# Weight splitting without a scaling pass and without a GpSimd subtraction, and a new table of ranks for the order of the work

## The chip, the cores and the metric

The kernel runs on one core of one Trainium2 chip. The core has five engines that run side by side, each through its own list of instructions in a fixed order: TensorE (PE, matrix products), VectorE (DVE) and ScalarE (ACT) for element-wise work, GpSimd (POOL), and SyncE (SP), which here only starts transfers (DMAs). Semaphores make an instruction wait for another engine's result. The metric is the time on the device of one execution, in microseconds (us); shown are the median of three timed executions and one more execution that was profiled.

## The reference

Two stages run one after the other. The first filters each of 8 sequences in the frequency domain; the second sends each of the 19968 rows through one of 8 small networks.

```python
# first stage: x is (8, 2496, 256)
X = np.fft.rfft(x, axis=1)
Yr = Xr @ w_r - Xi @ w_i + b_r
Yi = Xr @ w_i + Xi @ w_r + b_i
Yr, Yi = (sign(Y) * maximum(abs(Y) - 0.01, 0) for Y in (Yr, Yi))
y = np.fft.irfft(Yr + 1j * Yi, n=2496, axis=1)
# second stage: x = y as (19968, 256); w1 is (8, 256, 1024), w2 is (8, 1024, 256)
logits = x @ w_gate
e = argmax(logits, axis=1);  gate = softmax(logits)[row, e]
out[row] = gate * (maximum(x[row] @ w1[e], 0) @ w2[e])
```

## The kernel before, in words

Each sequence is a batch b of 0 to 7. Its transform of length 2496 is factored as 39 x 64, so that it is two matrix products in a row with a store to HBM and a load in another layout between them. Products that need more than half precision are made from a high and a low float16 part of each operand, three products instead of one.

The steps of a batch, with the lines of the functions and the engine: `s1` (L480, PE) is the first transform in six pieces, `s1_out` (L487, ACT) takes it from PSUM, `s1_store` and `zload` (L493, L498, SP) carry it through HBM. Then five pieces per batch run through a chain: `s2` (L509, PE); `s2_hi` (L514, ACT), `s2_lo` (L519, DVE) and `s2_neg` (L525, ACT), which split its result; `wmul` (L537 to L539, PE, 48 products), the weights of the filter; `thr` (L546, DVE), `thr_pos` (L552, ACT), `thr_sub` (L558, DVE), `thr_out` (L564, ACT) and `thr_lo` (L569, POOL), the threshold and the split for the way back; `inv1` (L585 to L587, PE), `inv1_hi` (L592, ACT), `inv1_lo` (L597, DVE), and `vstore` (L602, SP). When the five pieces of a batch are stored, `inv2` (L638, PE) makes the second inverse transform, `ytrans` and `logits` the gate's products, `route1` to `route3` find each row's expert and place, and 22 `scatter` instructions (L758, POOL) write the rows to HBM in the order of experts. `table` (DVE) then says which rows a block of 256 takes.

The second stage has 71 blocks of 256 rows and 21 of 128. A block is `fetch_x` (L944) and `fetch_w` (L935, the expert's weights, only where the expert changes), `up` (L980 to L982, 24 or 48 products), `up_relu` (ACT), `up_hi` and `up_lo` (DVE), `down` (L1008 to L1010, 24 products), `down_gate` (ACT) and `down_store` (L1019, POOL). Blocks 0 to 11 need batches 0 and 1, blocks 12 to 21 batch 2 as well, and so on; the first block can start when two batches are routed and all weights are split.

The weights of the 8 experts are split beside the first stage, in 16 units u of 1 MB: `wprep_load` (L778, SP), `wprep_sq` (L783, ACT, a sum of squares), `wprep_sum` (L787, PE), `wprep_scale` (DVE, a power of two), and for each half of the unit `wprep_mul` (L804, DVE: times the power of two, in place), `wprep_hi` (L808, ACT: the float16 part), `wprep_lo` (L812, POOL: the rest) and `wprep_store` (L817, SP).

The order on every engine is made before the program is built, by a planner (`Plan.run`): it keeps a list of ready tasks for each engine and starts the one of lowest rank when the engine is free, with a duration and buffers given for each task. A DMA of a rank above 0 waits while the modelled transfer queue is longer than `BACK`. The order that comes out is what the engines run; on the chip an engine that waits holds everything behind it. The load of weight unit u is not ready before `WT0 + WTD * u`, and the loads of the second inverse for batches from 2 on not before `INV0 + INVD * (b - 2)`.

Of the kernel before, what the change touches and what calls it, by code (L numbers as in the profile page):

```python
# [13 lines left out]
AF = mybir.ActivationFunctionType  # L14
ALU = mybir.AluOpType
# [17 lines left out]
def blocks(B):  # L33

    NT = B * NSEQ
    NF = -(-(NT - NE * 255) // 256)
    NB = NF + (NT + NE * 127) // 128 - 2 * NF
    tabs, j0 = [], 0  # L40
    for m, n in sorted(EPOCHS.items()):
        if m < B:
            tabs.append((m, j0, n - j0, 256))
            j0 = n
    tabs += [(B, j0, NF - j0, 256), (B, NF, NB - NF, 128)]
    slot, pos = [], []
    for t, (_, j0, n, _) in enumerate(tabs):
        k = KS if j0 >= JS else 2
        sl = [j % k for j in range(j0, j0 + n)]
        p, at = [0] * n, 0  # L50
        for s in range(k):
            own = [i for i in range(n) if sl[i] == s]
            for q, i in enumerate(own if t % 2 == 0 else own[::-1]):
                p[i] = at + q
            at += len(own)
        slot += sl
        pos += p
    return NF, NB, tabs, slot, pos
# [73 lines left out]
EPOCHS = {2:12,3:22,4:31,5:41,6:51,7:61}  # L132
JS, NPRE = 12, 2
SCD = 2.6
INV0, INVD, WT0, WTD = 430, 90, 60, 24
EV = -1
FILL = 430
ZD = 3
# [12 lines left out]
class Plan:  # L151


    LAT, DLAT, BACK = 0.2, 2.0, 4.0

    def __init__(self, bufs):
        self.t, self.bufs, self.mark = [], bufs, {}
# [2 lines left out]
        return Buf(name)  # L160

    def add(self, eng, dur, f, *a, deps=(), rank=0, take=(), free=(), dma=0.0, name=None, after=0.0, prev=None, lag=0.0):
        t = dict(eng=eng, dur=dur, f=f, a=a, deps=[d for d in deps if d is not None], rank=rank, take=take, free=free,
                 dma=dma, i=len(self.t), after=after, name=name, prev=prev, lag=lag)
        for b in free:
            b.left += 1
        self.t.append(t)
        if name is not None:
            self.mark[name] = t
        return t  # L170
# [86 lines left out]
def build(ctx: ExitStack, tc: tile.TileContext, x, w_r, w_i, b_r, b_i, wg, w1, w2,  # L257
# [3 lines left out]
    V, S, P, T, Q = nc.vector, nc.scalar, nc.gpsimd, nc.tensor, nc.sync  # L261
# [9 lines left out]
    NF, NB, TABS, SLOT, _ = blocks(B)  # L271
# [164 lines left out]
    st = {}  # L436
# [361 lines left out]
    def wparts_of(u, i):  # L798
        return (st[("ws", u)][:, 1024 * i:1024 * i + 1024],
                wt[u % 2][1][:, i, :].rearrange("p (l c) -> p l c", l=2))  # L800

    def wprep_mul(u, i):
        wi, _ = wparts_of(u, i)
        V.tensor_scalar(wi, wi, st[("wn", u)][:, 1:2], None, op0=ALU.mult)  # L804

    def wprep_hi(u, i):
        wi, wo = wparts_of(u, i)
        S.activation(wo[:, 0, :], wi, AF.Copy)  # L808

    def wprep_lo(u, i):  # L810
        wi, wo = wparts_of(u, i)
        P.tensor_tensor(wo[:, 1, :], wi, wo[:, 0, :], ALU.subtract)  # L812

    def wprep_store(u, i):
        e, w = divmod(u, 2)
# [213 lines left out]
    A = L.add  # L1029
# [44 lines left out]
    def ns_(c):  # L1074
        return min(4, SLOTS - 4 * c)
# [2 lines left out]
    wst_ = {}  # L1078
    for u in range(2 * NE):
        wa, wb = L.buf(f"wt{u % 2}0"), L.buf(f"wt{u % 2}1")  # L1080
        ld = A("SP", 1.0, wprep_load, u, take=[wa], dma=3.4, rank=0.5, after=WT0 + WTD * u)
        sq = A("ACT", 2.5, wprep_sq, u, deps=[ld], rank=0)
        sm_ = A("PE", 0.2, wprep_sum, u, deps=[sq, wst_.get(("sc", u - 1))], rank=-100)
        scl = wst_["sc", u] = A("DVE", 1.5, wprep_scale, u, deps=[sm_], rank=0, take=[wb])
        for i in range(2):
            m_ = A("DVE", 1.1, wprep_mul, u, i, deps=[scl], rank=0)
            h = A("ACT", 1.05, wprep_hi, u, i, deps=[m_], rank=0)
            l = A("POOL", 2.3, wprep_lo, u, i, deps=[h], rank=0, free=[wa])
            wst_[u, i] = A("SP", 0.5, wprep_store, u, i, deps=[l], dma=1.7, rank=0, free=[wb])
    wdone = [t for k, t in wst_.items() if k[0] != "sc"]  # L1090

# [1 line left out]
    for b in range(B):  # L1093
        F = 10 * b

        ld = [] if b else ld0
        for c in range(6):
            if b:
                ld.append(A("SP", 1.3, load_x, b, 4 * c, 4 * c + ns_(c), deps=[s1l[b - 1, c], nps[b - 1][c]],
                            rank=0.3, dma=8.0 * ns_(c) / 22))  # L1100
# [9 lines left out]
        for c in range(6):  # L1110
# [3 lines left out]
                              rank=F - 9.5, take=[pb_, zb] + ([zdb] if not c else []))  # L1114
            l = A("ACT", 1.05 * k, s1_out, b, c, deps=[t], free=[pb_], rank=EV)
# [3 lines left out]
        for i in range(5):  # L1119
# [3 lines left out]
            h = A("ACT", 1.11, s2_hi, b, i, deps=[t, xs], rank=EV)  # L1123
            l = A("DVE", 1.28, s2_lo, b, i, deps=[h], free=[p2_], rank=EV)
# [9 lines left out]
            h = A("ACT", 1.01, inv1_hi, b, i, deps=[v1], rank=EV)  # L1134
            l = A("DVE", 1.22, inv1_lo, b, i, deps=[h], free=[pa_], rank=EV)
# [10 lines left out]
        for c in range(6):  # L1146
# [5 lines left out]
                  take=[pb_, yr_], free=[vs_], rank=I + 2, lag=0.0 if pre else 6.0)  # L1152
            h = A("ACT", 1.12 * k, inv2_hi, b, c, deps=[t, ys], rank=EV)
            l = A("DVE", 1.28 * k, inv2_lo, b, c, deps=[h], free=[pb_], rank=EV)
# [39 lines left out]
    for j in range(NB):  # L1194
# [3 lines left out]
                       take=[xb_[j], tb_[j]], dma=1.95 if j < NF else 0.98, rank=0 if j < js else 1.2 + j * 1e-3, prev=ft.get(j - 1))  # L1198
        for w in range(2):
            wb_[j, w] = L.buf(f"wt{SLOT[j]}{w}")  # L1200
            wl[j, w] = A("SP", 0.8, fetch_w, j, w, deps=[tabs[ep]] + (wdone if j < 2 else []) + ([sw] if j >= js else []),
                         take=[wb_[j, w]], dma=1.3, rank=0 if j < js else 1.1 + j * 1e-3 + w * 5e-4,
                         prev=wl.get((j - 1, w)))
    for k, (kind, j, q) in enumerate(seq):
        if kind == "u":
# [3 lines left out]
            if q == 0:  # L1209
# [4 lines left out]
                             free=[xb_[j], wb_[j, 0]], rank=M + k)  # L1214
# [3 lines left out]
        else:  # L1218
# [3 lines left out]
                  free=hs_ + [wb_[j, 1]], rank=M + k)  # L1222
# [23 lines left out]
```

## Time and profile before

| | |
|---|---|
| timed executions | 1453.88, 1455.05, 1458.22 us; median 1455.05 us |
| profiled execution | 1445.12 us, span on the core 1442.9 us |
| PE busy | 1383.2 us, 96% of the span |
| DVE busy | 872.7 us, 60% |
| ACT busy | 696.8 us, 48% |
| POOL busy | 540.2 us, 37% |

The span is what lies between the first and the last instruction on the core; 2.2 us of the profiled execution lie around it. The profiled execution is 9.9 us under the median of the timed ones. The first block's `up` starts at 516.74 us; before that point the core works mainly on the first stage and the weights, after it mainly on blocks.

### The profile page before, as it was taken

Reading aid. Unit: us, or ns where it says so; the run is one execution under the profiler, and the core shown is the slowest. Engines: PE = TensorE matmul, PEld = TensorE weight load, DVE = VectorE, ACT = ScalarE, POOL = GpSimd, SP = SyncE. Lnnn points to the kernel's source line nnn. Section 1 sums busy time; section 2 is a strip of 40 time slices with the busy share of each in tenths; the row PEclk is TensorE's granted clock in tenths of the full one; section 3 lists DMA queues with packets and bytes.
Section 4 is the critical chain, followed back from the end, with each engine's and each line's share of the span. In section 5 each row is a group of like instructions: output and inputs, shape, how many; then the busy total and the mean of one; then the engine's idle time right before and its main releaser. Section 6 shows DMA issues by size and latency. Waiting matters only on the chain.

```text
span 1442.9 us, 33059 instructions
## 1 busy us (share of the span) xinstructions
PE 1383.2 (96%) x12682; PEld 1176.1 (82%) x12682; DVE 872.7 (60%) x1744; ACT 696.8 (48%) x909; POOL 540.2 (37%) x463
## 2 busy tenths in 40 slices
PE   6898999999978799999999999999999999999998
PEld 2687678778767688888888888888888888889997
DVE  3367687686679877566557567557568333343443
ACT  4688898898987452332333333332332222222222
POOL 0024142645455633643534534525524521111121
PEclk8999999999999899999999999999999999999999
DMA  8998889989877756776896978987784484676982
GB/s 230 273 312 273 280 250 283 301 296 299 285 241 236 248 143 177 199 184 222 259 272 205 289 218 234 261 207 232 218 243 134 134 245 118 191 209 214 204 199 102
DMA packets 228110, 329.06 MB, mean 228 GB/s; under 512 B 123637, under 2 KB 175255, under 8 KB 213232
## 3 DMA queue, kind: packets, MB, share of 16 engines
q1 hardware_dynamic: 211680, 285.86, 68.8%
q0 software_dynamic: 16272, 41.09, 8.3%
q8 instruction: 100, 1.64, 0.5%
q14 instruction: 58, 0.48, 0.1%
HBM read 277.28 MB, written 105.83 MB: 266 GB/s over the span
## 4 chain that ended last, share of the span: by engine, by line
PE 76%; DVE 7%; issue 6%; DMA 4%; ACT 3%; POOL 3%; SPq 1%; POOLq 0%; DVEq 0%; ACTq 0%
PE mm L980 9%; PE mm L982 9%; PE mm L981 9%; PE pob L1008 9%; PE pob L1009 9%; PE pob L1010 9%; PE mm L480 3%; PE mm L638 3%; PE mm L537 3%; PE mm L539 3%; PE mm L538 3%; PE mm L509 2%; POOL rows L758 1%; DMA x<-x 1%; DMA zs<-zd 1%
## 5 line engine op out<-in xcount | busy, mean ns | idle before, releaser
L980 PE MATMUL mm<-xt,wt 128*128 128x256 f16 (+1 forms) x1472 | 367.0, 260 | 0.0
L982 PE MATMUL mm<-xt,wt 128*128 128x256 f16 (+1 forms) x1472 | 367.0, 260 | 0.0
L981 PE MATMUL mm<-xt,wt 128*128 128x256 f16 (+1 forms) x1472 | 367.0, 260 | 0.0
L1019 POOL DMA_INDIRECT out<-o,ix x163 | 165.0, 1012 | 516.3 <-ACT o L1015 421.4
L1008 PE MATMUL pob<-wt,hh 128*128 128x256 f16 x1112 | 303.1, 273 | 0.6 <-ACT o L1015 0.6
L1010 PE MATMUL pob<-wt,hh 128*128 128x256 f16 x1112 | 303.1, 273 | 0.0
L1009 PE MATMUL pob<-wt,hh 128*128 128x256 f16 x1112 | 303.0, 273 | 0.0
L986 ACT ACTIVATE r<-mm 128x1024 f32<-128x1024 f32 x139 | 142.2, 1023 | 290.6 <-PE mm L982 265.3
L992 DVE CAST hh<-r 128x1024 f16<-128x1024 f32 x139 | 96.7, 696 | 245.5 <-ACT r L986 245.3
L758 POOL DMA_INDIRECT rows<-yr,ix x176 | 197.3, 1121 | 70.9 <-issue 62.4
L1015 ACT ACTIVATE o<-pob,g 128x256 f32<-128x256 f32 x163 | 75.9, 473 | 278.0 <-PE pob L1010 274.9
L569 POOL TENSOR_TENSOR sh<-u,sh 128x1024 f16<-128x1024 f32 x40 | 86.2, 2154 | 258.2 <-ACT sh L564 233.7
L537 PE MATMUL mm<-w,xa 128*128 128x256 f16 x640 | 175.6, 274 | 4.8 <-DVE vt L597 4.8
L538 PE MATMUL mm<-w,xa 128*128 128x256 f16 x640 | 175.6, 274 | 0.0
L539 PE MATMUL mm<-w,xa 128*128 128x256 f16 x640 | 175.6, 274 | 0.0
L997 DVE TENSOR_TENSOR hh<-r,hh 128x1024 f16<-128x1024 f32 x139 | 170.3, 1225 | 4.6
L980 PEld LDWEIGHTS <-wt 128*128 128x128 f16 x1472 | 143.9, 98 | 14.9
L981 PEld LDWEIGHTS <-wt 128*128 128x128 f16 x1472 | 144.0, 98 | 14.8
L982 PEld LDWEIGHTS <-wt 128*128 128x128 f16 x1472 | 144.0, 98 | 12.9
L1009 PEld LDWEIGHTS <-hh 128*128 128x128 f16 x1112 | 108.8, 98 | 14.6 <-issue 1.5
L1008 PEld LDWEIGHTS <-hh 128*128 128x128 f16 x1112 | 108.8, 98 | 13.9 <-issue 0.8
L1010 PEld LDWEIGHTS <-hh 128*128 128x128 f16 x1112 | 108.8, 98 | 12.6
(182 smaller groups left out, 2321.6 us busy)
## 6 DMA issues: line engine op xcount, KB each, us to landing
wt<-wsc SPq DMA_DIRECT2D x184, 1024.0 KB
zs<-zd SPq DMA_DIRECT2D x80, 256.0 KB
vd<-vt SPq DMA_DIRECT2D x80, 256.0 KB
vs<-vd SPq DMA_DIRECT2D x40, 480.0 KB
x<-x SPq DMA_DIRECT2D x40, 468.0 KB
zd<-zt SPq DMA_DIRECT2D x37, 480.0 KB
wt<-moe_w SPq DMA_DIRECT2D x32, 512.0 KB
wsc<-wt SPq DMA_DIRECT2D x32, 512.0 KB
```

Of the source, the lines that this page charges most:

```text
L537: T.matmul(o, lh, w16[:, r, h, 0, :], start=(h == 0 and r == 0), stop=False)
L538: T.matmul(o, lh, w16[:, r, h, 1, :], start=False, stop=False)
L539: T.matmul(o, ll, w16[:, r, h, 0, :], start=False, stop=(h == 1 and r == 1))
L758: i = P.indirect_dma_start(out=rows, out_offset=bass.IndirectOffsetOnAxis(ap=s["ix"][:, j:j + 1], axis=0), in_=s[("yr", j // 4)][:, j % 4, ...
L980: T.matmul(pv[:, a, :], wh, xt[:, h, :], start=(h == 0), stop=False)
L981: T.matmul(pv[:, a, :], wh, xt[:, 2 + h, :], start=False, stop=False)
L982: T.matmul(pv[:, a, :], wl, xt[:, h, :], start=False, stop=(h == 1))
L997: V.tensor_tensor(hh[:, :, 1, :], H.pop(("r", j, q)).rearrange("p (a n) -> p a n", n=n), hh[:, :, 0, :], ALU.subtract)
L1008: T.matmul(po, hi, wh, start=(fc == 0), stop=False)
L1009: T.matmul(po, hi, wl, start=False, stop=False)
L1010: T.matmul(po, lo, wh, start=False, stop=(fc == 7))
L1019: i = P.indirect_dma_start(out=out, out_offset=bass.IndirectOffsetOnAxis(ap=ix[:, t:t + 1], axis=0), in_=H.pop(("o", j, t)), in_offset=Non ...
```

## The change

Three things change. First, `wprep_mul` is gone: `wprep_hi` (ACT) takes the power of two as its scale, and `wprep_lo` moves from POOL to DVE as one instruction that multiplies the weights by the power of two and subtracts the high part. Second, each task's rank gets a number added that is looked up by the kind of task, and one that is looked up by kind and batch (or unit or block). Third, some constants of the planner differ. `max(0.0, ...)` is 0 for each of the 16 units, so that a weight load is ready from the start and goes when SP has nothing of a lower rank.

```diff
-INV0, INVD, WT0, WTD = 430, 90, 60, 24
+INV0, INVD, WT0, WTD, WT2 = 478.3, 108.66, -1095.76, 96.09, -109.51
+RANK = {"down": 3, "g_hi": 12.85, "g_lo": 16.3, "inv1": 0.15, "inv1.0": 9.9, "inv1.1": -5.8, "inv1.5": 44.85,
...
-    LAT, DLAT, BACK = 0.2, 2.0, 4.0
+    LAT, DLAT, BACK = 0.2, 2.0, 5.88
...
+        rank += RANK.get(f.__name__, 0) + (RANK.get(f"{f.__name__}.{a[0]}", 0) if a else 0)
...
-    def wprep_mul(u, i):
-        wi, _ = wparts_of(u, i)
-        V.tensor_scalar(wi, wi, st[("wn", u)][:, 1:2], None, op0=ALU.mult)
-
     def wprep_hi(u, i):
         wi, wo = wparts_of(u, i)
-        S.activation(wo[:, 0, :], wi, AF.Copy)
+        S.activation(wo[:, 0, :], wi, AF.Copy, scale=st[("wn", u)][:, 1:2])
 
     def wprep_lo(u, i):
         wi, wo = wparts_of(u, i)
-        P.tensor_tensor(wo[:, 1, :], wi, wo[:, 0, :], ALU.subtract)
+        V.scalar_tensor_tensor(wo[:, 1, :], wi, st[("wn", u)][:, 1:2], wo[:, 0, :], op0=ALU.mult, op1=ALU.subtract)
...
-        ld = A("SP", 1.0, wprep_load, u, take=[wa], dma=3.4, rank=0.5, after=WT0 + WTD * u)
+        ld = A("SP", 1.0, wprep_load, u, take=[wa], dma=3.4, rank=0.5, after=max(0.0, WT0 + WTD * u + WT2 * max(0, u - 8)))
...
-            m_ = A("DVE", 1.1, wprep_mul, u, i, deps=[scl], rank=0)
-            h = A("ACT", 1.05, wprep_hi, u, i, deps=[m_], rank=0)
-            l = A("POOL", 2.3, wprep_lo, u, i, deps=[h], rank=0, free=[wa])
+            h = A("ACT", 1.05, wprep_hi, u, i, deps=[scl], rank=0)
+            l = A("DVE", 1.3, wprep_lo, u, i, deps=[h], rank=0, free=[wa])
```

What this does to the order is shown at three places. The first is SP's queue of transfers near the start, from the first load of the constant `cd` to the first loads of `zs`, the input of `s2`. In it `x` is the input (a load of batch 1 from here on), `zd` the store of `s1`, and `wt<-moe_w` a weight load. Before:

```order
L332 DMA cd<-c_d 128x512
L493 DMA zd_107<-zt 120x1024 x2
L493 DMA zd_107<-yt 120x1024 x2
L493 DMA zd_107<-vs 120x1024
L493 DMA zd_107<-vs 120x512
L299 DMA x_92<-x 117x1x1024 x4
L332 DMA cd<-c_d 128x512
L498 DMA zs<-zd_107 64x4x256 x4
```

Now, the same queue from `cd` on, as far as the last stores of batch 0:

```order
L363 DMA cd<-c_d 128x512
L809 DMA wt_74<-moe_w 128x1024 x2
L809 DMA wt_76<-moe_w 128x4x256 x2
L330 DMA x_92<-x 117x1x1024
L524 DMA zd_107<-zt 120x1024
L330 DMA x_92<-x 117x1x1024 x2
L524 DMA zd_107<-zt 120x1024
L524 DMA zd_107<-yt 120x1024
L330 DMA x_92<-x 117x1x1024 x2
L333 DMA x_92<-x 39x512 x2
L524 DMA zd_107<-yt 120x1024
L524 DMA zd_107<-vs 120x1024
```

and then up to the first `zs`:

```order
L524 DMA zd_107<-vs 120x512
L524 DMA zd_108<-zt 120x1024
L330 DMA x_92<-x 117x1x1024 x2
L524 DMA zd_108<-zt 120x1024
L363 DMA cd<-c_d 128x512 x3
L529 DMA zs<-zd_107 64x4x256 x4
```

Two weight units, the rest of batch 1, two pieces of batch 2, two stores of batch 1 and two more pieces of `cd` now stand ahead of the first `zs`.

The second place is PE's list where batch 0's first `s2` and `wmul` stand (`mm<-cd,zs` is `s2`, `mm<-x,cc` is `s1`, two products of 512 columns to a piece, `sm<-wa` a `wprep_sum`). Before:

```order
L385 MATMUL sm<-acc,ones 128x3
L480 MATMUL mm<-x_92,cc 128x512 x4
L509 MATMUL mm<-cd,zs 128x128 x16
L480 MATMUL mm<-x_92,cc 128x512 x4
L537 LDWEIGHTS xa
L537 MATMUL mm<-w_121,xa 128x256
```

Now:

```order
L818 MATMUL sm<-wa,ones 128x2
L511 MATMUL mm<-x_92,cc 128x512 x4
L487 MATMUL sm<-a_278,ones 128x6
L818 MATMUL sm<-wa,ones 128x2
L511 MATMUL mm<-x_92,cc 128x512 x4
L540 MATMUL mm<-cd,zs 128x128 x16
L511 MATMUL mm<-x_92,cc 128x512 x2
L568 LDWEIGHTS xa
L568 MATMUL mm<-w_121,xa 128x256
```

More of `s1` stands ahead of the first `s2`, and only one piece of `s1`, instead of two, stands between the second `s2` and the first `wmul`.

The third place is POOL's list at the end of the first stage (`sh<-u,sh` is `thr_lo`, `rows<-yr,ix` a `scatter` of batch 1, `wt<-wt,wt` the old `wprep_lo`, `yr<-c` a small step of the second inverse). Before, from the last weight unit on:

```order
L812 TENSOR_TENSOR wt_77<-wt_76,wt_77 128x1024 x2
L758 DMA rows<-yr,ix 161792x516
L569 TENSOR_TENSOR sh<-u,sh 128x4x256
L758 DMA rows<-yr,ix 161792x516 x2
L658 TENSOR_SCALAR yr<-c_98 128x4
L758 DMA rows<-yr,ix 161792x516 x4
```

Now:

```order
L600 TENSOR_TENSOR sh<-u,sh 128x4x256
L789 DMA rows<-yr,ix 161792x516 x9
L600 TENSOR_TENSOR sh<-u,sh 128x4x256
L789 DMA rows<-yr,ix 161792x516 x5
L600 TENSOR_TENSOR sh<-u,sh 128x4x256
L789 DMA rows<-yr,ix 161792x516 x7
L600 TENSOR_TENSOR sh<-u,sh 128x4x256 x14
```

All scatters of batch 1 now stand ahead of the last 14 `thr_lo` of a row, up to nine of them between two `thr_lo`, and no weights are on POOL.

## Rows read from the trace of the kernel before

**Rows 1.** Busy time by stage: stretch, length, PE, PEld, DVE, ACT, POOL, PE clock, DMA.
```profile
0.00:41.26 41.26, 23.64 (x59) 9.80 (x59) 10.84 (x55) 20.87 (x35) 0.19 (x4) 0.88 0.85 237
41.26:120.00 78.74, 77.09 (x577) 63.30 (x578) 39.34 (x56) 62.83 (x78) 20.07 (x9) 0.98 0.90 285
120.00:400.00 280.00, 266.84 (x2120) 211.31 (x2119) 200.91 (x365) 246.10 (x322) 119.59 (x76) 0.98 0.89 284
400.00:516.74 116.74, 95.36 (x829) 79.35 (x827) 101.86 (x195) 80.49 (x101) 64.16 (x46) 0.93 0.74 234
516.74:1436.00 919.26, 918.28 (x9088) 810.80 (x9087) 519.73 (x1073) 286.08 (x375) 334.80 (x328) 1.00 0.74 206
```

**Rows 2.** Longest waits in 400 to 517 us that end on PE: waiter, releaser, total, times, longest.
```profile
PE mm L638 <- DVE u L546: 6.8, 1, 6.8
PE sm L787 <- ACT junk L783: 5.4, 1, 5.4
```

**Rows 3.** Groups by line: operation, count, busy us, mean ns, idle before.
```profile
L804 DVE TENSOR_SCALAR wt<-wt,wn 128x1024 f32<-128x1024 f32 x32 | 35.4, 1125 | 1.1 <-DVE wn L370 0.3 <-ACT junk L576 0.2
L812 POOL TENSOR_TENSOR wt<-wt,wt 128x1024 f16<-128x1024 f32 x32 | 75.2, 2363 | 48.8 <-ACT wt L808 43.6 <-DMA zs<-zd 2.9 <-DMA vd<-vt 2.3
L997 DVE TENSOR_TENSOR hh<-r,hh 128x1024 f16<-128x1024 f32 x139 | 170.3, 1225 | 4.6
L558 DVE SCALAR_TENSOR_TENSOR u<-u,sb,cl 128x1024 f32<-128x1024 f32 x40 | 56.2, 1405 | 10.4 <-ACT cl L552 10.4
L569 POOL TENSOR_TENSOR sh<-u,sh 128x1024 f16<-128x1024 f32 x40 | 86.2, 2154 | 258.2 <-ACT sh L564 233.7 <-DMA zs<-zd 10.4 <-DVE ix L963 6.9
L758 POOL DMA_INDIRECT rows<-yr,ix x176 | 197.3, 1121 | 70.9 <-issue 62.4 <-DVE base L751 6.6 <-DMA rows<-yr,ix 0.3
```

**Rows 4.** One line alone, L804: duration ns min/median/max.
```profile
L804 DVE TENSOR_SCALAR wt<-wt,wn x32: 737/753/2627, 85.7 to 462.3; 128x1024 f32<-128x1024 f32 x32
```

**Rows 5.** In order of time, DVE and POOL at 441 us: start, us.
```profile
441.37 2.58 DVE L558 SCALAR_TENSOR_TENSOR u<-u,sb,cl 128x1024 f32<-128x1024 f32 x1
440.74 5.21 POOL L812 TENSOR_TENSOR wt<-wt,wt 128x1024 f16<-128x1024 f32 x2 [2.89 <-DMA zs<-zd]
```

**Rows 6.** Transfers by kind: count, KB each.
```profile
wt<-moe_w SPq DMA_DIRECT2D x32, 512.0 KB
x<-x SPq DMA_DIRECT2D x40, 468.0 KB
zd<-zt SPq DMA_DIRECT2D x37, 480.0 KB
cd<-c_d SPq DMA_DIRECT2D x5, 256.0 KB
```

**Rows 7.** The stages of the start, as rows 1; the last number is GB/s.
```profile
4.00:16.00 12.00, 12.00 (x35) 5.08 (x33) 2.67 (x5) 5.94 (x8) 0.00 (x0) 1.00 0.89 247
18.00:26.00 8.00, 2.33 (x9) 0.94 (x7) 3.12 (x24) 3.84 (x9) 0.00 (x0) 0.93 0.91 320
```

**Rows 8.** In order of time, SP and PE at the first `s2`.
```profile
29.32 2.72 SPq L498 DMA_DIRECT2D zs<-zd  x4
41.26 5.43 PE L509 MATMUL mm<-cd,zs 128*128 128x128 f32 x32 [4.25 <-DMA zs<-zd]
46.53 3.60 PE L480 MATMUL mm<-x,cc 117*128 117x512 f32 x8
```

**Rows 9.** In order of time, ACT and DVE behind the first `s2`.
```profile
44.41 1.11 ACT L514 ACTIVATE xa<-mm,sb 128x1024 f16<-128x1024 f32 x1 [3.97 <-PE mm L509]
45.56 1.28 DVE L519 SCALAR_TENSOR_TENSOR xa<-mm,sb,xa 128x1024 f16<-128x1024 f32 x1 [15.79 <-ACT xa L514]
47.74 1.05 ACT L525 ACTIVATE xa<-xa 128x1024 f16<-128x1024 f16 x1
```

**Rows 10.** A stretch of blocks alone, as rows 1.
```profile
1240.00:1280.00 40.00, 40.00 (x369) 35.85 (x367) 16.49 (x24) 11.56 (x16) 7.25 (x8) 1.00 0.68 203
```

**Rows 11.** In order of time, the first fetch of a block on SP and its first product on PE.
```profile
510.48 1.37 SPq L944 DMA_TRANSPOSE xt<-rows  x1
516.74 0.27 PE L980 MATMUL mm<-xt,wt 128*128 128x256 f16 x1
```

More of the change, by code (lines that the diff above doesn't have):

```diff
@@ L134 @@
 SCD = 2.6
-INV0, INVD, WT0, WTD = 430, 90, 60, 24
+INV0, INVD, WT0, WTD, WT2 = 478.3, 108.66, -1095.76, 96.09, -109.51
+RANK = {"down": 3, "g_hi": 12.85, "g_lo": 16.3, "inv1": 0.15, "inv1.0": 9.9, "inv1.1": -5.8, "inv1.5": 44.85,
[4 rows of a table added]
+        "load_ce": 120.55, "load_rest": 39.2, "load_w": 4, "load_x": -48.85, "load_x.1": -2.3, "load_x.2": -8.45,
[18 rows of a table added]
+        "vstore.6": -5.25, "vstore.7": 63.95, "vzero": 10, "w_hi": -0.6, "warm": -4.6, "wmul": 99.2, "wmul.1": -8,
+        "wmul.3": -5.4, "wmul.4": -2.85, "wmul.6": 3.85, "wprep_hi": 121.55, "wprep_lo": 90.55, "wprep_load": 125.8,
+        "wprep_scale": 143.25, "wprep_sq": 427.85, "wprep_store": 139.45, "wscale": -0.6, "xscale": 3.4, "xscale.0": 11,
+        "xscale.1": -11.6, "xscale.6": 0.4, "xscale.7": 1.6, "ynorm": 142.95, "ytrans": -7.25, "ytrans.1": -11.85,
+        "ytrans.3": 2.3, "ytrans.4": 5.4, "zload.0": -2, "zload.1": 0.15, "zload.2": -1.05, "zload.5": 26.8,
+        "zload.6": 20.5, "zload.7": -0.85}
 EV = -1
```

22 rows, old and new, of the table RANK are left out of this document.

## The prediction

> **What bounds the kernel now.** I read the busy time by stage first. From 516.74 us on PE is busy 918.28 of 919.26 us [rows 1]: the blocks leave nothing to gain, and the span after that point is fixed by the number of products. Everything that the change can move lies before it. There PE is idle 17.6 us up to the first `s2` at 41.26 us, then 1.65, 13.16 and 21.38 us in the three stages that follow [rows 1]; the last 36.2 us together. PE also runs slower in them: the granted clock is 0.98, 0.98 and 0.93 (1.00 is 2.4 GHz; a mean below it holds short stretches at 1.2), and its lost shares of the busy time are 1.5, 5.3 and 6.7 us, 13.5 us in all, beside 1.00 in the blocks. So some 50 us of the 475.5 us between the first `s2` and the first block are lost. ACT is busy 82% and DVE 72% of that stretch (389 and 342 us), so neither is the bound by its sum; the waits come from the order. In the last stage DVE is busy 87%, and the two longest single waits that end on PE there are one for a DVE instruction of batch 2's second inverse, 6.8 us, and one for ACT's sum of squares of a late weight unit, 5.4 us [rows 2]. The waits of POOL for ACT are long in the list of groups, but POOL is idle anyway.
>
> **The start.** What the diff does not tell, the order does: two weight units, 4 x 512 KB, go into the transfer queue ahead of everything that `s2` needs, and with them the last pieces of batch 1 (468 KB and 2 x 78 KB, taken as 0.64 MB), two pieces of batch 2 (0.96 MB), two stores of batch 1 (0.98 MB) and two pieces of `cd` (0.52 MB) [rows 6]. With the weights' 2.10 MB these are 5.2 MB more. The queue is full there: it moved 247 GB/s while `x` was loaded and 320 GB/s while `zd` was stored [rows 7], and the first `zs`, issued at 29.32 us, let `s2` start only at 41.26 us [rows 8]. 5.2 MB take 16 us at the one rate and 21 at the other. I take 17, since stores and weights are the larger part, and the first `s2` comes near 58 us. PE does two more pieces of `s1` before it, 3.60 us [rows 8], and two small sums, 0.2 us. The loss on PE is 17 - 3.8 = 13 us; its bounds are 0, if the queue has gaps that the rows don't show, and 17.
>
> **The operations.** The 32 `wprep_mul` leave DVE: 32 x 1.125 = 36 us [rows 3]. The 32 `wprep_lo` leave POOL, 75 us, and come to DVE in a form that the trace does not have. The nearest rows are the subtraction L997, 1.225 us, and L558, 1.405 us, which reads two tiles and a column as the new one does [rows 3]; I take 1.25, the float16 result of L997, so 40 us, between 39 and 45. DVE gets 4 us more in 475, hidden by its 28% idle time. ACT's 32 copies gain a scale read from a column: L514 with one takes 1.11 us and L525 without 1.05 [rows 9], so 0 to 2 us, taken as 0. If these covers were gone, 4 us would count, in the last stage alone about 1.
>
> Beside a subtraction on POOL some DVE instructions stand still: an L558 of 1.28 us took 2.58 while POOL ran two subtractions [rows 5], and L804 has a mean of 1125 ns over a median of 753 [rows 3, 4], so 11.9 of its 36 us are such waits. POOL keeps 40 subtractions (L569), 86 us of the stretch. The Trainium skill, page "SBUF — State Buffer", section "Who interferes with whom", says that a DVE instruction with two inputs in SBUF contends with a GpSimd instruction that reads SBUF, and that the later one stops until the other is done. This speaks against the new `wprep_lo`, which has two such inputs; the L558 row agrees with it. By that rule 18% of 32 would start inside a POOL subtraction and wait half of 2.15 us, 6 us on DVE, and the sum below would be 10 instead of 11 us; without it 11.
>
> **The stretch up to the first block.** Three terms replace the 50 us.
>
> First, pairs of `s2` and `wmul`. What must lie between them is ACT's split, DVE's split and ACT's copy: from 44.41 us, when ACT starts, to 46.84, when DVE is done, 2.4 us, and the copy must be done six products into `wmul`, so about 3.1 us with free engines [rows 9]. I counted the products that stand between a piece's `s2` and its `wmul` in the order and gave each the trace's time (1.8 us for a piece of `s1` [rows 8], 0.109 us for a product of 256 columns, 40 us by 369 [rows 10]). Before, the least of 40 pairs has 5.2 us, and the median 24.6. Now 14 pairs have 5.0 us or less, six of them 3.1 to 3.2, and the median is 6.7. Each such pair has PE waiting when ACT or DVE has another instruction of 1.1 or 1.3 us in front: 0 to 2.4 us. I take 1.2 for the six and 0.5 for the other eight, 11 us, between 0 and 34.
>
> Second, the waits up to 400 us, 1.65 + 13.16 idle and 6.8 of clock, 21.6 us. The weight subtractions go from POOL, so `thr_lo` waits for fewer, but up to nine scatters now stand in a row ahead of one, 9 x (1.12 + 0.40) = 14 us [rows 3], and the products between that piece's `wmul` and `inv1` cover just about this. I keep 10 us, between 0 and 22.
>
> Third, the last stage, 21.38 + 6.7 = 28 us. Batch 1's routing and scatters have moved away: 160 us of PE work lie between its `route2` and the first block, where 54 us lay before. Batch 2's second inverse mostly moves behind the first block. Were DVE only as busy as in the stage before, PE would lose at that stage's rate, 18.5 in 280 us, so 7.7 in 116.74; I take 4, since the two waits of rows 2 are both of the moved kinds.
>
> **The blocks.** `down` after both `up` changes no count. The least work on PE between the product that frees a fetch and the fetch's use goes from 8.9 us (block 0; weights 10.5) to 12.0 (block 13). Block 0's fetch was issued 6.3 us before its use and made PE wait for nothing [rows 11]. Block 12's fetch now has 13.3 us of products, with up to three weight loads of 1 MB ahead of it, 3.1 to 4.2 us each at the rates of rows 7: a wait of 0 to 6 us, taken as 1.
>
> **Sum.** 13 - 50 + 11 + 10 + 4 + 1 = -11 us against the profiled 1445.12 us. The timed median is 1455.05 us, 9.9 above it; nothing in the profile tells where these lie, so I add the difference to the median: 1444 us.
>
> **Rivals.** (B) The pairs take over: PE finds ACT or DVE occupied at nearly each of the 14, 2.4 us each, 34 instead of 11: 1444 + 23 = 1467 us, slower. From 1.6 us per pair on (22 us) there is no gain left. For it: ACT is busy 246.1 of 280 us from 120 to 400 us [rows 1], so a free ACT is the exception. Against it: the planner's order puts ACT's split first among what is ready, and the wait is then half an instruction.
>
> (C) The pairs cost nothing: the order on ACT and DVE has each split just where the products end. 1444 - 11 = 1433 us, and with a start that loses only 4 us, 1424. For it: before, `wmul` of the first piece started on time with 5.2 us. Against it: 5.2 is more than 3.1.
>
> (D) The losses only change place: the stretch up to 400 us keeps 16 us and the last stage 7.7. Then 13 - 50 + 11 + 16 + 7.7 + 1 = -1 us, 1454 us. For it: PE's products and ACT's instructions are the same in number, and only DVE's backlog in the last stage is removed for certain.
>
> **Numbers.** The forecast (A) has a chance of 0.48, B 0.24, C 0.14, D 0.14. The likeliest's own range is 1437 to 1451 us. The range of 1424 to 1467 takes in C, D and the middle of B and leaves out the worse half of B and a faster C, less than 0.2 together. A measurement of this kernel can tell about 0.3%, 4.4 us. A and C are faster by more, 0.62; D is within, 0.14; B slower, 0.24.
>
> **What would show it.** The first `s2` near 58 us, and its wait ended by `zs`; were it near 45, the first term is wrong. PE idle from there to the first block about 25 us less lost clock, with waits of `wmul` for ACT's copy or DVE's split in a dozen places; if those waits are 2 us and more, B. The stage before the first block at less than 5 us of idle PE, with DVE under 80%. DVE's `wprep_lo` at 1.2 to 1.4 us, a few near 2.5. No idle PE from the first block on but for some us at block 12. If PE is idle more than 2 us in the later blocks, my count of what a fetch has is wrong.

## The result, and the profile after

The changed kernel takes 1473.78 us (median of 5 runs, 1465.76 to 1481.18) where the kernel before, beside it, takes 1455.05 (1453.81 to 1458.9): a ratio of 1.0123, 95% interval 1.0085 to 1.0161. I had forecast 1444 us, faster. But the ratio is not the same everywhere. Repeated on four chips, called A to D here, the same two kernels gave (the chip of the first result is not on record):

| chip | before, us | changed kernel | without the 3 on `down` | updates missing, before / changed |
|---|---|---|---|---|
| first result | 1455.05 | 1.0123 (1.0085 to 1.0161) | | 1* / 240 |
| A | 1456.22 | 1.0086 (1.0062 to 1.0110) | 0.9910 (0.9883 to 0.9937) | - / 244 |
| B | 1444.17 | 0.9900 (0.9861 to 0.9938) | 0.9872 (0.9837 to 0.9906) | 2 / 6 |
| C | 1453.84 | 1.0029 (1.0013 to 1.0045) | | 185 / 238 |
| D | 1456.51 | 1.0095 (1.0068 to 1.0122) | 0.9919 (0.9889 to 0.9949) | - / 246 |

The last column counts, in each profile, the ends of PE, ACT and DVE instructions that should raise a semaphore and have no update on record within 0.35 us, of some 2,800; some of these updates come later, others are not there at all. It splits the profiles in two groups with nothing between: 0 to 9 missing in all eight profiles of chip B, 185 to 355 in the eleven others of the changed kernel and the experiments. On B the change does what was forecast (1431.79 against 1444.17 us, -12.4; the forecast's sum was -11); elsewhere it does not, and on C, with as many missing as on A, it is slower by 0.3% only. The profile of before on which the prediction rests (*) has 1 missing and took 1445.12 us: it is like B, while the times shown beside it, 1453.88 to 1458.22, are like A, C and D.

The changed kernel by stage, as [rows 1], in the first result (updates missing):

```profile
0.00:51.52 51.52, 31.29 (x73) 13.45 (x73) 18.53 (x85) 33.82 (x55) 0.19 (x4) 0.80 0.85 288
51.52:120.00 68.48, 67.44 (x516) 54.62 (x516) 35.12 (x58) 56.77 (x74) 10.66 (x5) 1.00 0.94 303
120.00:400.00 280.00, 258.18 (x2062) 202.32 (x2062) 207.32 (x390) 232.19 (x300) 98.11 (x78) 0.98 0.83 262
400.00:511.12 111.12, 106.14 (x907) 92.01 (x904) 80.93 (x124) 91.28 (x111) 26.60 (x14) 0.98 0.79 249
511.12:1456.00 944.88, 926.92 (x9117) 809.36 (x9116) 527.24 (x1091) 278.48 (x372) 325.46 (x328) 1.00 0.73 204
```

and on chip B, the same program:

```profile
0.00:52.22 52.22, 30.34 (x72) 13.19 (x73) 19.63 (x85) 35.41 (x57) 0.19 (x4) 0.84 0.85 284
52.22:120.00 67.78, 66.91 (x509) 55.23 (x510) 32.23 (x51) 53.40 (x69) 10.66 (x5) 0.97 0.91 297
120.00:400.00 280.00, 269.46 (x2187) 214.52 (x2186) 219.81 (x406) 246.87 (x317) 100.66 (x80) 0.99 0.88 280
400.00:495.69 95.69, 90.70 (x789) 79.35 (x788) 71.32 (x112) 79.20 (x95) 23.52 (x13) 1.00 0.79 237
495.69:1426.00 930.31, 922.61 (x9130) 810.97 (x9129) 525.88 (x1092) 279.89 (x372) 338.50 (x328) 1.00 0.77 207
```

Two rows differ. From 120 to 400 us PE is idle 21.8 us in the one and 10.5 in the other, and the first block comes 15.4 us later. In the blocks PE is idle 18.0 and 7.7 us (before: 1.0 [rows 1]). The last stage before the first block is as forecast in both: 5.0 us idle with DVE at 73 and 75%, where before it was 21.38 at 87%.

PE's longest wait between the first `s2` and the first block, 9.4 us, shows what is different. The last product of `inv1` that ACT's `inv1_hi` (L623) needs, and ACT from 338 us, in the first result (start, us):

```profile
340.43 0.27 PE L618 MATMUL mm<-sh,ce 128*128 128x256 f16 x1
```
```profile
338.69 1.06 ACT L814 ACTIVATE junk<-wt 128x1024 f16<-128x1024 f32 x1
...
340.23 1.11 ACT L545 ACTIVATE xa<-mm,sb 128x1024 f16<-128x1024 f32 x1 [0.40 <-PE mm L540]
349.09 1.02 ACT L623 ACTIVATE vt<-mm 128x1024 f16<-128x1024 f32 x1 [7.75 <-remote]
```

and POOL beside it, the first two and the last of a row of nine scatters:

```profile
337.30 1.00 POOL L789 DMA_INDIRECT rows<-yr,ix  x1 [0.17 <-issue]
338.61 0.97 POOL L789 DMA_INDIRECT rows<-yr,ix  x1 [0.31 <-issue]
...
347.55 0.97 POOL L789 DMA_INDIRECT rows<-yr,ix  x1 [0.30 <-issue]
```

The same instructions of ACT on chip B, beside the same nine scatters (334.43 to 345.75 us there):

```profile
335.80 1.06 ACT L814 ACTIVATE junk<-wt 128x1024 f16<-128x1024 f32 x1
...
336.86 1.09 ACT L545 ACTIVATE xa<-mm,sb 128x1024 f16<-128x1024 f32 x1
337.85 1.02 ACT L623 ACTIVATE vt<-mm 128x1024 f16<-128x1024 f32 x1
339.64 1.11 ACT L545 ACTIVATE xa<-mm,sb 128x1024 f16<-128x1024 f32 x1 [0.76 <-PE mm L540]
```

On B, ACT goes straight on. In the first result it stands 7.75 us, to 0.57 us after the last scatter ended, and the profile finds nobody who released it ("remote"): the update of the semaphore that it waits for is on record at 349.07 us, 8.4 us after PE's product ended. Not every signal is held: DVE's split of L545's result starts at 341.71 us, 0.4 us after L545 ended and in the middle of the row. `wmul` waits behind ACT: the waits of L568 for ACT's copy are, first in the first result, then on B (total, times, longest):

```profile
PE mm L568 <- ACT xa L556: 14.7, 7, 9.4
```
```profile
PE mm L568 <- ACT xa L556: 7.6, 8, 1.9
```

In the blocks the same happens in little. In the first result ACT's `up_relu` (L1013, written to `r`) has waits that end without a releaser ("remote"), 43.6 us in 12, on B none; and PE stumbles in `down` while POOL has six transfers in a row (705 to 713 us). ACT, then PE there:

```profile
709.21 1.02 ACT L1013 ACTIVATE r<-mm 128x1024 f32<-128x1024 f32 x1 [3.55 <-issue]
714.35 1.02 ACT L1013 ACTIVATE r<-mm 128x1024 f32<-128x1024 f32 x1 [4.12 <-remote]
```
```profile
711.61 0.27 PE L1036 MATMUL pob<-wt,hh 128*128 128x256 f16 x1
...
712.07 0.27 PE L1037 MATMUL pob<-wt,hh 128*128 128x256 f16 x1 [0.19 <-issue]
...
712.77 0.28 PE L1035 MATMUL pob<-wt,hh 128*128 128x256 f16 x1 [0.44 <-issue]
...
713.51 0.27 PE L1037 MATMUL pob<-wt,hh 128*128 128x256 f16 x1 [0.34 <-issue]
...
714.20 0.28 PE L1035 MATMUL pob<-wt,hh 128*128 128x256 f16 x1 [0.42 <-issue]
```

A product should follow every 0.109 us [rows 10]; here steps of up to 0.7 us cost 2.0 us, and about as much again near 823, 930 and 1143 us, each time some 6 us into a row of six. I call the first of the two "late signals": an engine has ended an instruction, and one that waits for it learns it late, in the case shown only when POOL is through. PE's stumbles are another thing: these products wait for no semaphore and raise none, so that a late signal cannot hold them, and what does is not known. They go together with the missing updates: in the eleven profiles with 185 and more missing, 1 to 52 products of the blocks that wait for no semaphore come after more than 0.15 us of idle PE (0.9 to 29.5 us in all), 188 of 196 during an indirect transfer or within 1 us after it; in the eight of chip B and in the first profile of before there is none.

Of the 18.0 us that PE is idle in the blocks of the first result, 7.7 are such stumbles and 6.9 are waits for ACT's `down_gate`, 4.6 of them in one place, where ACT waited for a store to land (on B the longest of PE's waits for it is 1.2 us):

```profile
PE pob L1035 <- ACT o L1042: 6.9, 6, 4.6
```
```profile
ACT o L1042 <- DMA out<-o,ix: 6.7, 1, 6.7
```

### The profile page after: what moved, and what is told of

Its sections match the earlier page's. It is cut to its first block, busy times and chain, and to the rows that moved or that the text cites. A ratio compares the mean times of both kernels' runs of the same rounds, so it can differ in the third digit from the quotient of the medians.

```text
span 1463.9 us, 32912 instructions
## 1 busy us (share of the span) xinstructions
PE 1391.7 (95%) x12682; PEld 1173.0 (80%) x12682; DVE 869.1 (59%) x1744; ACT 693.4 (47%) x909; POOL 463.1 (32%) x431
## 4 chain that ended last, share of the span: by engine, by line
PE 73%; issue 9%; ACT 5%; DVE 4%; DMA 4%; POOL 3%; another core or an unknown queue 1%; SPq 1%; POOLq 0%; ACTq 0%; DVEq 0%
PE mm L1007 8%; PE mm L1008 8%; PE mm L1009 8%; PE pob L1035 8%; PE pob L1036 8%; PE pob L1037 8%; PE mm L568 4%; PE mm L569 4%; PE mm L570 4%; PE mm L511 3%; PE mm L669 3%; PE mm L540 2%; POOL rows L789 2%; DMA out<-o,ix 1%
## 5 line engine op out<-in xcount | busy, mean ns | idle before, releaser
L1013 ACT ACTIVATE r<-mm 128x1024 f32<-128x1024 f32 x139 | 142.2, 1023 | 292.1 <-issue 121.9
L1042 ACT ACTIVATE o<-pob,g 128x256 f32<-128x256 f32 x163 | 70.1, 471 | 296.1 <-PE pob L1037 282.2
L568 PE MATMUL mm<-w,xa 128*128 128x256 f16 x640 | 176.4, 276 | 20.1 <-ACT xa L556 14.7
L1035 PEld LDWEIGHTS <-hh 128*128 128x128 f16 x1112 | 108.8, 98 | 18.8 <-issue 5.4
```

The lines of the kernel that those rows point to most:

```text
L568: T.matmul(o, lh, w16[:, r, h, 0, :], start=(h == 0 and r == 0), stop=False)
L1035: T.matmul(po, hi, wh, start=(fc == 0), stop=False)
```

## The experiments

All ratios are to the kernel before on the same chip. The theories: (1) the order of two ups and two downs costs the blocks their time; (2) the loss comes from where the late second inverses and scatters stand; (1a, 1b) in theory 1 it is POOL's rows of transfers that hold PE, or the order by itself; (3) the loss needs something that only some chips have; (4) that is late signals beside POOL's indirect transfers; (5) POOL has nothing to do with it.

**Chip A: undo one part, or do one alone.** `a_again` has no edit.

> The changed kernel once more, nothing edited. Its first profile lost some 24 us of PE time in the blocks, in pieces of about 2 us in which PE waited for nothing that the profile shows. If these belong to the program (theories 1 and 2), they are there again at the same blocks, and the time is 1468 to 1478 us. If they belong to one execution, the blocks lose less than 8 us or lose it elsewhere.

1470.42 us, 1.0086. Its six largest losses in the blocks are among the seven largest of the first result, at the same places of the program to within four of PE's instructions, so they belong to the program and not to one execution.

```diff
-RANK = {"down": 3, "g_hi": 12.85, ...
+RANK = {"g_hi": 12.85, ...
```

> The changed kernel without the 3 on the rank of down, so that up and down alternate again in most blocks. Theory 1 (two ups and then two downs cost the block stage its 24 us): about 1450 us, PE idle in the blocks under 5 us. Theory 2 (the loss comes from where the late batches' second inverses and scatters now stand, two pieces of inv2 in a row): 1468 to 1478 us, the losses stay.

1445.98 us, 0.9910: 24.4 us under the changed kernel. The waits of PE in the blocks, of the changed kernel and of this one:

```profile
PE pob L1035 <- ACT o L1042: 6.7, 4, 5.3
PE pob L1037 <- issue: 3.2, 7, 0.9
PE pob L1036 <- issue: 3.1, 6, 0.9
PE pob L1035 <- issue: 2.2, 4, 0.9
```
```profile
PE mm L1007 <- issue: 1.0, 4, 0.3
PE pob L1037 <- DVE xa L1024: 0.9, 1, 0.9
PE pob L1035 <- ACT o L1042: 0.7, 2, 0.6
```

The next has the new `wprep` functions and nothing else of the change (no `RANK`, the old constants).

> The kernel before with the new wprep code alone: no ranks, the old constants. By the prediction's terms the operations cost nothing by themselves: 1450 to 1458 us. If the loss comes from the operations (scaled copy on ACT, wprep_lo on DVE), 1470 or more.

1449.79 us, 0.9950 (0.9929 to 0.9972), about 6 us under before. That this is a gain of the operations is not shown: the first block starts at 516.83 us, no earlier than in the profiles of before (516.74 at first, 514.88 on chip C), and as far as profiles of different chips compare, the gain lies in the blocks (925.4 us from first product to last, 932.5 for before on C), where none of the new operations runs and only the order can differ.

```diff
     def add(self, eng, dur, f, *a, ...
+        rank += 3 if f.__name__ == "down" else 0
```

> The kernel before with 3 added to the rank of down and nothing else. Theory 1: 1475 to 1480 us, PE idle in the blocks near 24 us. Theory 2: 1453 to 1458 us.

1463.54 us, 1.0049 (1.0031 to 1.0067), 7.3 us over before: the sign of theory 1, a third of its size, and in neither range. So far theory 1 leads.

**Chip B, first set.** The kernel before alone:

> The kernel before once more, for a profile from the same chip as the others. In the other profiles PE stumbles (2 to 4 products in 2 us that wait for nothing the profile shows) about where POOL has six or more indirect transfers behind one another, and ACT's relu starts up to 4.3 us after its products ended. If this belongs to the chains of POOL (theory 1a), it is here too where scatters stand in fours (near 565, 600 and 670 us), and costs under 8 us in the blocks, since POOL's chains are short elsewhere.

1446.08 us in the one execution; no late relu, no update missing, though its scatters stand in fours. This chip does not show what chip A showed, and so it could not test 1a as meant.

```diff
-SCD = 2.6
+SCD = 1.3     # in the changed kernel without the 3 on down
```

> The changed kernel without the 3 on down (alternating up and down) and with SCD 1.3 for 2.6: the planner now puts three or four scatters of a late batch between two stores, where it put one or two. Theory 1a (PE is held while POOL runs a chain of indirect transfers; two ups and two downs only make the chains longer, because two stores then come together): the blocks lose 10 to 25 us again though the order alternates, 1456 to 1471 us. Theory 1b (the order of up and down costs by itself, through relu and its buffers): the same as without the 3, 1444 to 1448 us.

1439.66 us, 0.9982 (0.9964 to 1.0000). POOL runs up to 30 transfers in a row, no update is late, and no product stumbles: that POOL holds PE directly is not seen on this chip. But the rows are not free. The same kernel with SCD 2.6 has 0.9872 on this chip in the second set below, 14.5 us less, and its blocks take 921.4 us, where these take 935.0. By the ratio this is near the 1.000 to 1.010 that theory 1a's times stand for on chip A, and outside 1b's 0.992 to 0.994. PE's losses in the blocks, 10.3 us, are nearly all waits for DVE, and DVE waits longer for the stores of blocks (`out`) to land; its waits before L990 in the blocks, here and with SCD 2.6 (from 495 us on; total, times, longest):

```profile
DVE ix L990 <- DMA out<-o,ix: 107.5, 36, 7.5
```
```profile
DVE ix L990 <- DMA out<-o,ix: 56.7, 29, 4.6
```

That stores stand behind scatters on POOL, and so DVE behind the stores, fits these rows; it was not tested alone.

```diff
-SCD = 2.6
+SCD = 3.2     # in the changed kernel
```

> The changed kernel, two ups and two downs, with SCD 3.2 for 2.6: the scatters stand further apart, at most three in a row and mostly one or two. Theory 1a: the blocks lose clearly less, 8 to 16 us instead of 25, 1456 to 1464 us. Theory 1b: no change, 1468 to 1474 us.

1478.68 us, 1.0256, with PE waiting 22.3 us for `ytrans` and 10.4 for rows of a fetch: the value makes another, worse plan, so this tells nothing on scatters. Neither theory forecast it.

```diff
-INV0, INVD, WT0, WTD = 430, 90, 60, 24
+INV0, INVD, WT0, WTD = 478.3, 108.66, 60, 24     # new wprep code, no ranks
```

> The kernel before with the new wprep code and the changed kernel's INV0 and INVD (second inverses of late batches later), no ranks. By the prediction's third term the stage before the first block gets most of its 28 us back, since batch 2's second inverse moves behind the first block: 1432 to 1440 us. If the ranks are needed for it, 1448 to 1455 us, the same as the code alone.

1438.99 us, 0.9971 (0.9951 to 0.9991). It lies in the first range, but the absolute bounds were meant for chip A; by the ratio it is no better than the code alone had on chip A. Its first block starts at 500.3 us, against 512.3 in the profile of before, but its blocks take 4.6 us longer: part of what moving the inverse gains is given back.

**Chip B, second set.** Now the changed kernel beside its own version without the 3:

> The changed kernel a third time, beside its own version without the 3 on down. On the chip where it was slower by 0.9%, ACT's relu started up to 4.3 us late at 40 places and PE stumbled at 9; on the chip of the last four kernels neither was seen in any profile. Theory 1b (the order of ups and downs costs on every chip): 14 us or more above before, whatever chip this is. Theory 3 (the loss needs the late relus, which belong to one chip): where the profile has none, at most 5 us above before or below it; where it has them, 14 us above.

> The changed kernel without the 3 on down, again, beside it on the same chip. Theory 1b: 20 to 26 us under the changed kernel and 8 to 14 under before. Theory 3: 20 to 26 us under the changed kernel only where the profiles have late relus, else within 8 us of it.

> The kernel before, one look, for the profile on this chip. If the late relus belong to the chip, they are here too or missing in all four profiles.

1431.79 us (0.9900), 1425.13 us (0.9872), and 1446.67 us for the one execution of before; no late relu in any. Theory 1b is refuted as the main cause: two ups and two downs cost 6.7 us here, not 24. Theory 3 stands.

> The changed kernel without the 3 on down and with SCD 3.2: the partner of the run with SCD 3.2 and the 3, which was 2.6% slower than before and lost 45 us in the blocks, half of it in PE waiting for ytrans. Theory 1b and 2 differ here: if the 3 on down costs also in that plan, this is 20 us or more under that ratio (at most 1.010 of before); if SCD 3.2 alone made the plan bad, it stays above 1.015.

1469.80 us, 1.0172: SCD 3.2 alone makes the plan bad.

**Chips C and D: POOL's transfers doubled.** `b_extra` and `b_extra2` are the kernel before with

```diff
+        for to, l in ((out, scat2), (more, scat3)):     # more: a scratch tensor
             i = P.indirect_dma_start(out=to, ...
```

> The kernel before, with each indirect store of a block issued a second time, into a scratch tensor: 163 more indirect transfers on POOL, about 1 us each, while POOL is idle over 60% of the time; nothing waits for them but the buffer of the result. Theory 4 (on one chip the signals of PE, ACT and DVE reach the waiting engine late while POOL issues an indirect transfer, on the other not): where the profiles have late relus, 10 to 30 us slower than before, with more late relus; where they have none, within 5 us of before. Theory 5 (the late signals come with the chip, whatever POOL does): within 5 us of before on both.

> The changed kernel, beside the last one on the same chip. Theory 4: where its profile has late relus, 1.008 to 1.013 of before; where it has none, 0.986 to 0.994.

> The kernel before, one look. On a chip with late signals it shows for the first time what they cost before: by theory 4 some 10 us, of which most is where scatters of batches 2 and later stand in fours, and in the stage with the scatters of batch 1 (400 to 517 us).

Chip C: 1501.24 us (1.0309, 1.0266 to 1.0353), 1457.09 us (1.0029), 1454.57 us. Signals are late on C, also in the kernel before (185 updates missing). With the stores doubled 348 are missing, and PE's waits without a releaser in the blocks go from 3.3 to 29.5 us (25.7 of them before products that wait for no semaphore), these on top:

```profile
PE pob L1010 <- issue: 6.8, 11, 1.0
PE pob L1009 <- issue: 5.3, 9, 1.0
PE mm L983 <- issue: 4.7, 8, 1.0
```

Theory 4 has the sign; its 10 to 30 us were too few for 47, and its 1.008 to 1.013 for the changed kernel too many for 1.0029, with 238 missing: how many are missing does not tell what they cost. The 10 us that before was to take more are there against chip B, but in the blocks (925.0 to 932.5 us) and not in the stage from 400 us (28.1 to 29.1 us lost). Theory 5 is refuted if the transfers' own traffic is not the cause, which these runs on chip D were to tell:

> The kernel before with its block stores issued twice, once more. On a chip with late signals this was 3.1% slower. If that came from the late signals (theory 4), it is within 1% of before on a chip where no signals are late, and 2.5 to 3.5% slower on one where they are. If it comes from 21 MB more of traffic or from POOL's time, 2.5 to 3.5% on either.

> The changed kernel without the 3 on down, on the same chip: 0.987 to 0.995 of before with late signals or without.

> The changed kernel on the same chip: with late signals 1.002 to 1.013 of before, without 0.986 to 0.994; 5 to 10 us above the version without the 3 on down where none are late, and more where they are.

1507.06 us (1.0331), 1447.17 us (0.9919), 1468.90 us (1.0095). Signals were late on D too, so the doubled stores were never run where none are late. In all eleven profiles with late signals 99 to 100% of the missing updates lie between the start of an indirect transfer on POOL and 1 us after its end, a time that holds 31 to 44% of all updates. That they go together is shown. That POOL's issuing is what holds the signals back is argued from this, and from the 7.75 us above most of all; what else of 163 more transfers costs time was not separated, and why chip B has none of it stays open. A rival stands untested: every execution here has a span and a clock on record, so no run tells whether the recording itself, which loses the updates, takes part in the delay.

## Why the prediction was wrong

**The step that failed** is "The blocks" (+1), and behind it the choice of rows there and in "Second, the waits up to 400 us", and the line that carried the sum to the timed runs: "nothing in the profile tells where these lie, so I add the difference to the median". From the profile of before to that of the first result the blocks go from 921.3 to 946.6 us, 25 us where I had 1, and the first block starts 5.6 us earlier, where the other terms give 12. The 9.9 us were not a constant to add. They fit what the kernel before takes more where signals are late (B to C: 1444 to 1454 us, 7.5 us of it in the blocks, since its first block starts at 514.5 and 514.9 us), and the changed kernel loses more there: its blocks take 946.6 to 948.7 us in the first result and on A and D (936.9 on C, 930.7 on B). I looked at the row of nine scatters and counted only what waits behind it on POOL; "POOL is idle anyway" was my reading of its busy time.

Term by term, lost PE time (idle and clock) before and now: from the profile of before (1 update missing) to the first result (240), on chip B, and on chip C:

| term | forecast | first result | B | C |
|---|---|---|---|---|
| up to the first `s2` | +13 | 20.5 to 26.5, +6 | 22.3 to 26.7, +4 | 17.9 to 28.3, +10 |
| first `s2` to 400 us, pairs included | 21 left | 21.7 to 28.0 | 19.0 to 16.1 | 19.2 to 31.8 |
| 400 us to the first block | 4 left | 28.1 to 7.1 | 28.1 to 5.0 | 29.1 to 5.2 |
| blocks, first product to last | +1 | 921.3 to 946.6, +25 | 925.0 to 930.7, +6 | 932.5 to 936.9, +4 |
| first block starts earlier by | 12 | 5.6 | 18.8 | 3.5 |

On B the total, -12.4 us for -11, fits better than its terms: the start cost 9 us less than forecast, the blocks and what follows their last product 6 us more. That the sum came out is partly luck.

*The start.* The volume was right, the rate not. Up to the first `s2`, 14.8 MB moved now (288 x 51.52) and 9.8 before (237 x 41.26), 5.1 more for my 5.2; but from 26 us on the queue moved 323 to 346 GB/s now and 245 to 254 before, so that the first `s2` came at 51.5 instead of 58 us. I had allowed for less ("if the queue has gaps") and took 13 of 17. Nor was the wait all for `zs`, as I had it: the sum of squares of batch 1 (L487) now stands ahead of `s2` on PE, and PE's longest wait there is for ACT's part of it (8.5 us on B, with 3.5 for `zs`). In the first result (total, times, longest):

```profile
PE sm L487 <- ACT junk L483: 9.8, 2, 9.5
...
PE mm L540 <- DMA zs<-zd: 1.8, 1, 1.8
```

*The operations.* `wprep_lo` on DVE has a median of 1.28 us for my 1.25, 41.5 us in all. Before, of the DVE instructions that started inside a POOL subtraction, L558, with two tiles in SBUF, was held in 5 of 7 cases, and L804, with one tile and a column there, in 9 of 12; the four that read PSUM (L519, L546, L597, L652) never, in 36. Now 2 of 32 `wprep_lo` start inside one, and 1 is held, 2.71 us. The Trainium skill's rule (page "SBUF — State Buffer", section "Who interferes with whom") that a DVE instruction with two inputs in SBUF contends with a GpSimd instruction that reads SBUF, by which I priced a second case at 6 us, agrees with L558 and `wprep_lo`, though not each of them was held; 2 starts in 32 are fewer than the 18% of that case. And DVE's other instructions meet fewer subtractions: L558, mean 1405 ns [rows 3], is L589 now, 1278 ns.

```profile
L589 DVE SCALAR_TENSOR_TENSOR u<-u,sb,cl 128x1024 f32<-128x1024 f32 x40 | 51.1, 1278 | 10.4 <-ACT cl L583 10.3
...
L839 DVE SCALAR_TENSOR_TENSOR wt<-wt,wn,wt 128x1024 f16<-128x1024 f32 x32 | 41.5, 1324 | 9.4 <-ACT wt L835 8.5 <-DMA zd<-zt 0.8
```

ACT's copies with the scale take 1141 ns instead of 1048, 3 us in all where I had at most 2.

*The pairs.* Right where nothing is late: 8.7 us of waits of `wmul` for ACT's copy or DVE's split on chip B, in 10 places, for 11. (By [rows 9] a pair needs 2.43 + 1.05 - 6 x 0.109, 2.8 us, where I had written 3.1.) In the first result 15.5, of which 9.4 is the one wait behind the nine scatters. My rival B had the right sign there with the wrong agent: not ACT's other work, but a signal that comes late, makes that pair wait.

*The last stage.* Right: 5.0 us for 4 on B and 5.2 on C (7.1 in the first result, 2.1 of it clock), DVE under 80% on every chip.

*The blocks.* "`down` after both `up` changes no count" was true and not enough. The order costs 6.7 us in the whole kernel on chip B and 24.4 and 21.7 on A and D: ACT now takes both halves of a block's result together, so that the two stores stand together on POOL with the scatters behind them, and rows of five and more POOL instructions without a pause go from 9 in the blocks (profile before) to 33; without the 3 they are 11 (chip A). On chip A the changed kernel has 34 such rows and 20 stumbles of PE, the 3 alone in the kernel before 34 and 19, and the changed kernel without the 3 has 11 and 4. That this is the way from the order to the loss is argued from those counts; 1a was only tested where nothing is late. "If PE is idle more than 2 us in the later blocks, my count of what a fetch has is wrong" named the wrong suspect: no wait for a fetch is among the long ones.

## What to carry to other kernels

Before a sum is made from a profiled execution, ask why its time is not that of the timed ones: 9.9 us that no row explains is a cost that the change can multiply. An engine that is idle most of the time (POOL, busy 37%) may still be the one that holds others up, so what stands around a row of its instructions belongs in the sum: count the rows of indirect transfers before and after a reordering. Whether breaking them up helps is not shown: with SCD 3.2, on chip B, it made a worse plan. Try a reordering on more than one chip, and each of its parts alone: here one number in the table of ranks cost 7 to 24 us, and the version without it is the fastest of the three wherever it ran (0.987 to 0.992 of before, where the changed kernel has 0.990 to 1.010).

## What was not expected of the hardware

On three of four chips, and in the first result, semaphore updates of PE, ACT and DVE beside POOL's indirect transfers are missing from the record or late in it (185 to 355 of some 2,800 in a profile, against 0 to 9 on the fourth), and engines that wait for them start late: beside a row of nine scatters of 0.97 us each ACT stood for 7.75 us, to 0.57 us after the end of the row. In the same profiles PE stands before products that wait for no semaphore, beside the same transfers. On the fourth chip neither is seen, with rows of up to 30 transfers, though the plan with such rows is 14.5 us slower there than its partner. The kernel before, with nothing changed, takes 1443 to 1444 us on that chip and 1454 to 1457 on the others.
